# Memory attention with masked probabilities as the weights of the values product, and a ones column for the row sums

## The chip, the cores and the metric

The kernel runs on one core of a Trainium2 chip. The metric is the time of one execution on the device in microseconds (us). The time before is the median of three runs, 1568.24 us (1566.88 to 1571.79). A profile shows one execution, instruction by instruction; its span runs from the first to the last instruction.

## The reference

Two blocks alternate over x (2048 tokens of 512 numbers), each twice: A, B, A, B. Each is added to its input after a layer norm. Everything is stored in bf16.

```
def A(x, mem0):                       # 32 heads of 128, 64 segments of 32 tokens, 8 memory tokens
    mem = mem0
    for s in range(64):
        h = concat([mem, x[32 * s:32 * s + 32]])          # 40 tokens
        q, k, v = h @ Wq, h @ Wk, h @ Wv                  # per head
        scores = q @ k.T * 128 ** -0.5
        scores = where((idx[:, None] < 8) | (idx[:, None] >= idx[None, :]), scores, -1e9)
        o = (softmax(scores) @ v) @ Wo                    # summed over the heads
        mem = o[:8]                                       # memory of the next segment
        outs.append(o[8:])

def B(x):                             # linear attention, 32 heads of 16
    q, k, v = split(x @ wqkv); pq, pk = phi(q), phi(k)    # phi: t + 1 above 0, else exp(t), + 1e-6
    return (pq @ (pk.T @ v)) / (pq @ sum(pk) + 1e-6) @ wo
```

A memory token sees all 40 tokens, the others see those up to themselves. The memory makes the 64 segments of an A block a chain: segment s + 1 can't start its projections before segment s has its first 8 output rows.

## The kernel before, in words

**Blocks and segments.** `a_layer(0)` and `a_layer(1)` are the two A blocks, with 64 segments each. The B block of the tiles (128 tokens) is worked on beside them, by `b_in` (keys, values, sums) during the same layer and `b_out` (the result) during the next one; `b_mid` stands between. The weights Wq, Wk, Wv, Wo of A stay in SBUF.

**One segment.** Its tokens are 8 of memory and 24 new ones (`hT`); the last 8 tokens of each segment, the "left" ones, are projected for four segments at once (`left_block`, `left_values`: `vleft`). Heads are worked on in two halves `b`, four of them in four groups of 32 partitions each. `project` makes K, Q and V with 512-wide matmuls, four side by side in the four column parts of TensorE. `turned` evacuates K and Q and transposes them on VectorE in 32 x 32 blocks (line 2179). V is evacuated to `vimg`.

**Attention of the memory rows** (`mem_attention`, twice a segment, not in the last one: 252 times). The scores of all tokens lie in PSUM with the key tokens on the partitions (lines 2286 and 2294). ScalarE takes Exp (2301 for the memory rows, 2305 for the rest); VectorE spreads the memory rows' probabilities over the four parts with a mask (`Pm`, 2309). The row sums come from a matmul with a matrix of ones (`sums`), and ScalarE turns them into reciprocals with Ln and Exp (2320, 2322). The product takes the values as weights and the probabilities as moving data (`pvm`, through `tiled`, line 2060); VectorE multiplies it by the reciprocals into `oTb` (2334).

**Attention of the other rows** (`x_attention`, once a segment: 128 times). A mask (2352), sums by blocks with matmuls (2363, 2048), Ln and Exp (2366, 2368), scaling of the probabilities (2370, 2371), their spreading (`Pbx` 2374, `Pbl` 2379), the product with the values as weights (2060), and evacuations to `oTb` and `oTl` (1925 on ScalarE, 1926 on VectorE).

**Out.** `out_proj` multiplies `oTb` with Wo in 64 matmuls 256 wide (2424), adds the two halves of the heads (an evacuation to `outW`, and 2435), `next_mem` picks the memory rows (2452) and `residual` sends the other rows to `dx_sb` by DMA (1942), half of them through POOL's queue and half through SP's.

**Order.** Each instruction is a node with a key (layer, segment, name, number). A table `PLACE` gives each node a place in one list for all engines and, for those that ScalarE or VectorE can do (`ANY`, `evac`), the engine: "a" or "v". `schedule` sorts by it, gives out the eight PSUM banks and puts a semaphore wait where a node needs another engine's result. Each engine works through its part of the list in order, so an instruction that waits holds up everything behind it on its engine. Before, the numbers in the table are nanoseconds of a plan:

```
    (0, 10, 'mem0'): '155353 155412 155784 155903 156052 156645 157234 157542 157516 157918',
```

Of the kernel before, what the change touches and what calls it, by code (L numbers as in the profile page):

```python
# [6 lines left out]
F32 = mybir.dt.float32  # L7
F32R = mybir.dt.float32r
ACTF = mybir.ActivationFunctionType
ALU = mybir.AluOpType  # L10
# [1789 lines left out]
def _build_kernel(nc, A_x, A_mem0, A_Wq, A_Wk, A_Wv, A_Wo, A_seg_len, B_wqkv, B_wo, out):  # L1800
# [47 lines left out]
    st_sb = sb("st_sb", [128, 2, 16], F32)  # L1848


    ARENA_N = 35344
    arena = sb("arena_sb", [128, ARENA_N])
    off = [0]

# [1055 lines left out]
```

## Time and profile before

| | |
|---|---|
| Median of three runs | 1568.24 us (1566.88 to 1571.79) |
| Span of the profiled execution | 1565.9 us |
| Around the span, by the median of the runs | 2.3 us |
| Instructions in the profile | 97,746 |
| PE / PEld / DVE / ACT / POOL busy | 1514.7 / 822.9 / 1223.1 / 990.8 / 196.6 us |
| Granted TensorE clock | 0.998 |
| First 50 us: loading of the weights | 346 GB/s |
| Layers: stretches 50 to 770 and 810 to 1510 us | 720 and 700 us for 62 or 63 segments each |

The page has no time of the profiled execution other than its span; what lies around it is worked out from the runs. PE is TensorE's matmuls, PEld its weight loads, DVE VectorE, ACT ScalarE, POOL GpSimd and SP the queue of SyncE. A row of a group gives the line, the engine, the operation, out<-in by the names of the tiles, out<-in in partitions x elements, the count, and behind the bar the busy time in us and the mean of one in ns, then the idle time of the engine before them and what ended it. A row of the timeline gives the start in us, how long it took, and the count of merged instructions. `pb` is PSUM; `arena_sb` holds most of the tiles above. The records of instructions overlap: the next one may begin in its engine's pipe before the one before it has ended.

### The profile page before, as it was taken

What the parts mean: (1) busy time and instruction counts of PE and PEld (TensorE: products, weight loads), DVE (VectorE), ACT (ScalarE), POOL (GpSimd) and SP (SyncE); (2) the same over time, 40 slices, a digit from 0 to 9 for tenths busy, and PEclk for the clock granted to TensorE, in tenths of its full rate; (3) what the DMA queues carried; (4) which work ended last, traced back from release to release, by engine and by line L of the source; (5) the groups of instructions that cost most, each with busy time, mean ns of one, the idle gap of its engine ahead of it and who ended that gap; (6) DMA issues with size and microseconds to landing.
All of it is one profiled execution on the core that took longest, in us unless ns stands there. A gap on an engine that the chain in (4) does not pass through costs nothing.

```text
span 1565.9 us, 97746 instructions
## 1 busy us (share of the span) xinstructions
PE 1514.7 (97%) x48653; PEld 822.9 (53%) x40845; DVE 1223.1 (78%) x3520; ACT 990.8 (63%) x3059; POOL 196.6 (13%) x396
## 2 busy tenths in 40 slices
PE   6999999999999999999999999999999999999997
PEld 3455555555555555555545555555555555555454
DVE  4677878887777778777887878788888778777867
ACT  2566666666676666565666667656676666676666
POOL 2011110111111011111111110111111011111010
PEclk9999999999999999999999999999999999999999
DMA  9311000101000010101311100111001010111134
GB/s 383 96 31 21 23 28 20 27 24 24 24 17 14 23 25 23 25 17 32 54 38 20 24 21 19 30 27 27 18 20 27 24 26 20 27 23 17 27 55 130
DMA packets 84869, 60.72 MB, mean 39 GB/s; under 512 B 64169, under 2 KB 78825, under 8 KB 82921
## 3 DMA queue, kind: packets, MB, share of 16 engines
q1 hardware_dynamic: 71144, 37.58, 9.5%
q0 software_dynamic: 13152, 16.75, 3.8%
q8 instruction: 351, 5.75, 1.5%
q14 instruction: 62, 0.50, 0.1%
q10 hardware_dynamic: 160, 0.14, 0.0%
HBM read 25.57 MB, written 11.67 MB: 24 GB/s over the span
## 4 chain that ended last, share of the span: by engine, by line
PE 87%; DVE 7%; ACT 3%; DMA 2%; issue 1%; SPq 0%; POOL 0%; DVEq 0%; POOLq 0%
PE pb L2160 32%; PE pb L2048 21%; PE pb L2424 18%; PE pb L2060 10%; PE pb L2603 2%; DVE arena_sb L1926 2%; PE pb L2286 1%; DMA dx_sb<-y_sb 1%; ACT arena_sb L1925 1%; PE pb L2363 1%; PE pb L2452 1%; DVE y_sb L2435 1%; DVE arena_sb L2179 1%; DVE st_sb L2098 1%; ACT outW_sb L1925 1%
## 5 line engine op out<-in xcount | busy, mean ns | idle before, releaser
L1925 ACT ACTIVATE arena_sb<-pb 128x512 bf16<-128x512 f32 (+5 forms) x1175 | 527.7, 481 | 314.7 <-PE pb L2048 144.5
L2160 PE MATMUL pb<-Wk_sb,arena_sb 128*32 128x512 bf16 x4192 | 363.3, 380 | 1.8 <-DVE arena_sb L1926 1.1
L1926 DVE CAST arena_sb<-pb 128x512 bf16<-128x512 f32 (+4 forms) x598 | 302.0, 514 | 79.2 <-PE pb L2048 40.3
L2424 PE MATMUL pb<-Wo_sb,arena_sb 128*32 128x256 bf16 x10368 | 338.2, 273 | 5.8 <-issue 2.3
L2179 DVE STREAM_TRANSPOSE arena_sb<-arena_sb 128x256 f32<-128x256 f32 x640 | 266.4, 433 | 56.9 <-ACT arena_sb L1925 49.8
L2424 PEld LDWEIGHTS pb<-Wo_sb,arena_sb 128*32 128x32 bf16 x10368 | 258.4, 96 | 48.4 <-DVE arena_sb L2334 15.9
L2060 PE MATMUL pb<-arena_sb 128*32 128x128 bf16 (+2 forms) x10800 | 267.6, 208 | 11.2 <-DVE arena_sb L1926 3.9
L1942 POOL DMA_DIRECT2D dx_sb<-y_sb x246 | 124.8, 511 | 1146.1 <-DVE y_sb L2435 675.2
L2160 PE MATMUL pb<-Wq_sb,arena_sb 128*32 128x512 bf16 x3088 | 258.9, 380 | 1.1 <-issue 0.3
L2060 PEld LDWEIGHTS pb<-arena_sb 128*32 128x32 bf16 x10800 | 186.9, 95 | 135.9 <-issue 29.3
L2160 PE MATMUL pb<-Wv_sb,arena_sb 128*32 128x512 bf16 x2560 | 252.2, 380 | 0.0
L2048 PE MATMUL pb<-Wv_sb,arena_sb 128*32 128x512 bf16 x2560 | 252.1, 380 | 0.0
L2160 PEld LDWEIGHTS pb<-Wk_sb,arena_sb 128*32 128x32 bf16 x4192 | 112.3, 96 | 190.4 <-issue 99.4
L2048 PE MATMUL pb<-Wq_sb,arena_sb 128*32 128x512 bf16 x2032 | 198.9, 379 | 0.0
L2160 PEld LDWEIGHTS pb<-Wq_sb,arena_sb 128*32 128x32 bf16 x3088 | 83.8, 96 | 95.3 <-issue 42.0
L1925 ACT ACTIVATE outW_sb<-pb 64x256 f32<-64x256 f32 x137 | 51.7, 377 | 109.3 <-PE pb L2424 94.4
L2334 DVE TENSOR_TENSOR arena_sb<-pb,arena_sb 128x128 bf16<-128x128 f32 x252 | 73.2, 291 | 42.5 <-ACT arena_sb L2322 14.0
L2435 DVE TENSOR_TENSOR y_sb<-pb,outW_sb 64x256 bf16<-64x256 f32 x162 | 68.7, 424 | 46.4 <-ACT outW_sb L1925 41.3
L2374 DVE TENSOR_TENSOR arena_sb<-arena_sb,bo_sb 128x512 bf16<-128x512 bf16 x256 | 102.8, 416 | 2.4
L2160 PEld LDWEIGHTS pb<-Wv_sb,arena_sb 128*32 128x32 bf16 x2560 | 70.3, 96 | 56.5 <-issue 32.8
L2048 PE MATMUL pb<-Wk_sb,arena_sb 128*32 128x512 bf16 x928 | 92.4, 379 | 0.0
L2305 ACT ACTIVATE arena_sb<-pb 128x160 bf16<-128x160 f32 x256 | 77.4, 305 | 15.6 <-PE pb L2286 7.9
(129 smaller groups left out, 1816.3 us busy)
## 6 DMA issues: line engine op xcount, KB each, us to landing
Wk_sb<-in_A_Wk_dram SPq DMA_DIRECT2D x1, 4096.0 KB, 13.4
Wq_sb<-in_A_Wq_dram SPq DMA_DIRECT2D x1, 4096.0 KB, 24.0
Wv_sb<-in_A_Wv_dram SPq DMA_DIRECT2D x1, 4096.0 KB, 33.6
Wo_sb<-in_A_Wo_dram SPq DMA_DIRECT2D x16, 256.0 KB, 7.4
xs_scratch<-x_sb POOLq DMA_DIRECT2D x32, 128.0 KB, 2.1
pq_scratch<-arena_sb POOLq DMA_DIRECT2D x27, 128.0 KB, 2.8
x_sb<-xs_scratch POOLq DMA_DIRECT2D x16, 128.0 KB, 2.3
dx_sb<-y_sb POOLq DMA_DIRECT2D x126, 12.0 KB, 1.7
```

What stands on the lines that cost most here:

```text
L1925: return e.activation(o() if callable(o) else o, i() if callable(i) else i, ACTF.Copy)
L1926: return e.tensor_copy(o() if callable(o) else o, i() if callable(i) else i)
L1942: add(eng, lambda e: e.dma_start(o, i), 0.55 if eng == "pool" else 0.66, reads=reads, writes=writes, dsem="%s%d" % (kind, k), lat=lat + (0 ...
L2048: return pe.add_instruction(mybir.InstMatmult(name=nc.get_next_instruction_name(), engine=mybir.EngineType.PE, ins=[pe.lower_ap(x), pe.low ...
L2060: r = pe.matmul(o[q], w[:, q], x, start=start, stop=stop, skip_group_check=True, tile_position=(0, 32 * j))
L2160: r = pe.matmul(o, blk[:, c, :], w, start=(c == 0), stop=(c == 3), tile_position=(0, 32 * j))
L2179: add("dve", lambda v: v.transpose(dst, src(img[:, k, :].bitcast(F32))), 0.445, reads=[("img", k, h) for h in range(2)], writes=[dkey])
L2305: add("act", lambda a: a.activation(PQ[:, r2, b, 64:224], tl.f32()[:, 64:224], ACTF.Exp, scale=SCALE), c_act(160), tiles=[tl], writes=[("P ...
L2334: add("dve", lambda v: v.tensor_tensor(oTb[:, s % NO, 16 * b:16 * b + 16, 0:8].rearrange("p (i j) q -> p j i q", i=4), heads(pv.f32()[:, 0 ...
L2374: add("dve", lambda v, b=b: v.tensor_tensor(Pbx[:, :, b, :].rearrange("p j (k x) -> p j k x", k=4), px[:, b, :].rearrange("p (k x) -> p k ...
L2424: r = pe.matmul(tl.f32()[32 * j:32 * j + 32, 0:256], oT[:, 4 * hh + n, :], Wo_sb[:, 8 * n + hh, 256 * d:256 * d + 256], start=(hh == 0 and ...
L2435: add("dve", lambda e: e.tensor_tensor(y, tl.f32()[a, 0:256], outW[c, v, :], ALU.add), c_dve(256), reads=[("outW", w), "y0"], tiles=[tl], ...
```

## The change

The row sums come along with the product. V's tiles get two more columns of ones per head (`vimg`, `vleft`: 130 columns for 128), set once by POOL. The product is turned round: the masked probabilities are the weights, 32 columns for each of the four column parts, and the values with their ones columns move, 130 wide. Its result has the tokens on the partitions and the row sum in column 128. VectorE takes the reciprocal of that column, VectorE or ScalarE scales the result by it (`scaled`), and VectorE transposes the scaled result in 32 x 32 blocks into `oTb` or `oTl`. The sums by matmuls, Ln, Exp and the spreading of scaled probabilities go; one mask of 640 columns for each half (`wx_sb`) takes the place of the mask, the scaling and the spreading. Wo is loaded in the order that the transposed result asks for, in 32 DMAs for 16, and `out_proj` reads its weights at every second element. `PLACE` is a new list: ranks in place of nanoseconds, with another order of all work and other choices between ScalarE and VectorE.

```
-    (0, 10, 'mem0'): '155353 155412 155784 155903 156052 156645 157234 157542 157516 157918',
...
+PLACE: 1538 entries with ranks from 0 to 13499
...
-    vimg = av(2 * 1024).rearrange("p (r x) -> p r x", r=2)
+    vimg = av(2 * 8 * 130).rearrange("p (r n x) -> p r n x", r=2, n=8)
+    vleft = av(2 * 8 * 130).rearrange("p (r b g d) -> p r b g d", r=2, b=2, g=4)
...
+    for b in range(2):
+        for j in range(4):
+            u = 16 * b + 4 * j
+            for i in range(4):
+                load(Wo_sb[32 * i:32 * i + 32, u:u + 4, :].rearrange("p (f e) m -> p f (e m)", f=2),
+                     A_Wo[8 * j + 4 * b + i].rearrange("(f x e) m -> x f (e m)", f=2, e=2), ("Wo", b, j, i),
...
         # mem_attention
-            add("pe", sums, 0.112, reads=[("Pm", k), "one"], tiles=[tl])
-            add("act", lambda a: a.activation(Rm[:, k, :], tl.f32()[:, 256:384], ACTF.Ln), c_act(128), tiles=[tl],
-            add("act", lambda a: a.activation(Rm[:, k, :], Rm[:, k, :], ACTF.Exp, scale=-1.0), c_act(128, 0, 1),
...
+            def pvm(pe):
+                for a, start in ((0, True), (1, False)):
+                    for i in range(4):
+                        w = Pm[:, k, 128 * a + 32 * i:128 * a + 32 * i + 32]
+                        m = vimg[:, r2, 4 * b + i, :] if a else vleft[:, g2, b, g, :]
+                        r = pe.matmul(pv.f32()[32 * i:32 * i + 32, 0:130], w, m, start=start, stop=not start, skip_group_check=True,
+                                      tile_position=(0, 32 * i))
+            add("dve", lambda v: v.reciprocal(rc, pv.f32()[:, 128:129]), 0.17, tiles=[pv], writes=[("Rm", k)])
+            scaled(omem[:, k, :].unsqueeze(1), lambda: pv.f32()[:, 0:128].unsqueeze(1), rc, 1, [("Rm", k)], [pv], [("om", k)])
+            add("dve", lambda v: v.transpose(oTb[:, s % NO, b, :, :, 0].rearrange("p h j q e -> p (h j) (q e)").bitcast(F32),
+                                             omem[:, k, :].bitcast(F32)), 0.232, reads=[("om", k)], writes=[("oTm", s % NO, b)])
+        def scaled(o, i, r, n, reads, tiles, writes):
+            def fn(e):
+                if hasattr(e, "activation"):
+                    for u in range(n):
+                        x = e.activation(o[:, u, :], i()[:, u, :], ACTF.Copy, scale=r[:, u:u + 1])
+                    return x
+                return e.tensor_tensor(o, i(), r.unsqueeze(2).to_broadcast([128, n, 128]), ALU.mult)
...
         # x_attention
+            for b in range(2):
                 add("dve", lambda v, b=b: v.tensor_tensor(
+                    Px[:, b, :].rearrange("p (n j x) -> p n j x", n=20, j=4),
+                    PQ[:, r2, b, 64:224].rearrange("p (n x) -> p n x", n=20).unsqueeze(2).to_broadcast([128, 20, 4, 8]),
+                    wx_sb[:, :].rearrange("p (n j x) -> p n j x", n=20, j=4), ALU.mult),
+            cols = lambda b, k, i: Px[:, b, 128 * k + 32 * i:128 * k + 32 * i + 32]
...
+                        for i in range(4):                      # for k in range(3), b in range(2)
+                            r = pe.matmul(pv.f32()[32 * i:32 * i + 32, 130 * k:130 * k + 130], cols(b, k, i),
+                                          vimg[:, r2, 4 * b + i, :], start=True, stop=True, skip_group_check=True,
...
+                scaled(ox, lambda pvv=pvv: pvv()[:, :, 0:128], rc, 3, [("Rx", b)], [pv], ["ox"])
...
+                    for k in range(3, 5):                       # the left rows, both halves in one bank
+                        for i in range(4):
+                            r = pe.matmul(pv.f32()[32 * i:32 * i + 32, 130 * b:130 * b + 130], cols(b, k, i),
+                                          vleft[:, g2, b, g, :] if k == 4 else vimg[:, r2, 4 * b + i, :], start=k == 3, stop=k == 4,
...
+            scaled(oleft, lambda: pvv()[:, :, 0:128], rc, 2, ["Rl"], [pv], ["ol"])
...
         # out_proj
-                            r = pe.matmul(tl.f32()[32 * j:32 * j + 32, 0:256], oT[:, 4 * hh + n, :],
+                            r = pe.matmul(tl.f32()[32 * j:32 * j + 32, 0:256], oT[:, b, f, n, :, :, e],
```

The built programs differ in these counts: TensorE 48,647 to 42,583 instructions, VectorE 3,522 to 4,108, ScalarE 3,063 to 2,634, POOL 400 in both, SP 376 to 392.

More of the change, by code (lines that the diff above doesn't have):

```diff
@@ L1962, in _build_kernel @@
         load(W[:, :, :], v, nm, t)
-    for i in range(4):
-        for n in range(4):
-            hs = slice(8 * n + 2 * i, 8 * n + 2 * i + 2)
-            load(Wo_sb[:, hs, :], A_Wo[hs].rearrange("h e d -> e h d"), ("Wo", i, n), 36.45 + 3.0 * i + 0.75 * n, "dWo%d" % i)
+    for b in range(2):
[4 more added lines that the diff above has]
+                     A_Wo[8 * j + 4 * b + i].rearrange("(f x e) m -> x f (e m)", f=2, e=2), ("Wo", b, j, i),
+                     36.45 + 6.0 * b + 1.5 * j + 0.375 * i, "dWo%d%d" % (b, j))
     P.count += 1
@@ L2313, in mem_attention @@
+                wm_sb[:, :].rearrange("p (n j x) -> p n j x", n=8, j=4), ALU.mult),
                 c_dve(256, 2), reads=[("PQm", r2, b), "wm"], writes=[("Pm", k)])
[L2315 to L2321 removed]
@@ L2344, in x_attention @@
             gl = slice(8 * g, 8 * g + 8)
-            pxl = PQ[:, r2, :, 64:224]
-            px = PQ[:, r2, :, 64:192]
-            p8 = PQ[:, r2, :, 192:224]
-            rx = Rx.rearrange("p (b x) -> p b x", b=2)
             pk = [("PQ", r2, 0), ("PQ", r2, 1)]
-            tl = P.tile()
-            add("dve", lambda v: v.tensor_tensor(pxl, pxl, mx_sb[:, :].unsqueeze(1).to_broadcast([128, 2, 160]), ALU.mult),
-                c_dve(320, 2), reads=pk + ["mx"], writes=[("Px", r2)])
-            def sums(pe):
-                for left in range(2):
-                    for j in range(4):
-                        q = slice(32 * j, 32 * j + 32)
-                        o = tl.f32()[q, 0:256].rearrange("p (b x) -> p b x", b=2)
-                        if left:
-                            r = again(pe, o[:, :, 96:128], bo_sb[:, q], p8, False, True, (0, 32 * j))
-                        else:
-                            pe.matmul(o, bo_sb[:, q], px, start=True, stop=False, tile_position=(0, 32 * j))
-                return r
@@ L2365, in x_attention @@
-            add("pe", sums, 0.137, reads=[("Px", r2), "bo"], tiles=[tl])
-            add("act", lambda a: a.activation(Rx, tl.f32()[:, 0:256], ACTF.Ln),
-                c_act(256), tiles=[tl], writes=["Rx"])
-            add("act", lambda a: a.activation(Rx, Rx, ACTF.Exp, scale=-1.0), c_act(256, 0, 1),
-                reads=["Rx"], writes=["Rx"])
-            add("dve", lambda v: v.tensor_tensor(px, px, rx, ALU.mult), c_dve(256), reads=["Rx"], writes=[("Px", r2)])
-            add("dve", lambda v: v.tensor_tensor(p8, p8, rx[:, :, 96:128], ALU.mult), c_dve(64),
-                reads=pk + ["Rx", ("Px", r2)], writes=[("PL", r2)])
+            last = s == NSEG - 1
@@ new lines, in x_attention @@
+                pvv = lambda pv=pv: pv.f32()[:, 0:390].rearrange("p (k x) -> p k x", k=3)
+                rc = Rc[:, 2 + 3 * b:5 + 3 * b]
+                add("dve", lambda v, rc=rc, pvv=pvv: v.reciprocal(rc.unsqueeze(2), pvv()[:, :, 128:129]), 0.18, tiles=[pv], writes=[("Rx", b)])
+                scaled(ox, lambda pvv=pvv: pvv()[:, :, 0:128], rc, 3, [("Rx", b)], [pv], ["ox"])
+                k0 = 0 if last else 1
+                add("dve", lambda v, b=b, k0=k0: v.transpose(
+                    oTb[:, s1, b, :, :, k0:k0 + 3].rearrange("p h j k q e -> p k (h j) (q e)").bitcast(F32),
+                    ox.rearrange("p k x -> p (k x)").bitcast(F32)), 0.366, reads=["ox"],
+                    writes=[("oTx", s1, b)] + ([("oTm", s1, b)] if last else []))
@@ new lines, in x_attention @@
+            pvv = lambda pv=pv: pv.f32()[:, 0:260].rearrange("p (b x) -> p b x", b=2)
+            rc = Rc[:, 8:10]
+            add("dve", lambda v: v.reciprocal(rc.unsqueeze(2), pvv()[:, :, 128:129]), 0.17, tiles=[pv], writes=["Rl"])
+            scaled(oleft, lambda: pvv()[:, :, 0:128], rc, 2, ["Rl"], [pv], ["ol"])
+            dst, wr = (oTb[:, s1, :, :, :, 3], []) if last else (oTl[:, g2, :, :, :, g], [("oTl", g2, b) for b in range(2)])
+            if last:
+                wr = [("oTx", s1, b) for b in range(2)]
@@ L2410, in out_proj @@
+            add("dve", lambda v: v.transpose(dst.rearrange("p b h j q e -> p b (h j) (q e)").bitcast(F32), oleft[:, :, :].bitcast(F32)),
+                0.3, reads=["ol"], writes=wr)
         def out_proj(oT, keys, urgent, end=False):
@@ L2422, in mm @@
                             k, d = divmod(j, 2)
-                            n = 2 * k + i
-                            r = pe.matmul(tl.f32()[32 * j:32 * j + 32, 0:256], oT[:, 4 * hh + n, :],
-                                          Wo_sb[:, 8 * n + hh, 256 * d:256 * d + 256], start=(hh == 0 and i == 0),
+                            n, f, e = 2 * k + (u + i) // 4, (u + i) // 2 % 2, (u + i) % 2
+                            r = pe.matmul(tl.f32()[32 * j:32 * j + 32, 0:256], oT[:, b, f, n, :, :, e],
+                                          Wo_sb[:, 16 * b + 4 * n + 2 * f + e, 256 * d:256 * d + 256], start=(hh == 0 and i == 0),
                                           stop=(hh == 7 and i == 1), tile_position=(0, 32 * j))
                     return r
-                add("pe", mm, 0.218, reads=[("Wo", hh // 2, n) for n in range(4)] + keys[hh // 4], tiles=[tl])
+                add("pe", mm, 0.218, reads=[("Wo", hh // 4, 2 * k + hh // 2 % 2, i) for k in range(2) for i in range(4)] + keys[hh // 4], tiles=[tl])
             k = int(w == NW - 1)
@@ L2467, in left_rows @@
         def left_rows(G):
[L2468 removed]
+            k = out_proj(oTl[:, G % 2], [[("oTl", G % 2, b)] for b in range(2)], False)
             rows_out(k, G, [(8 * g, 32 * g + 24, 8) for g in range(4)])
@@ L2524, in tokens @@
                 x_move(x_sb[:, slot(t), :], x_view[t], slot(t), [], [("x", slot(t))], "dxl", lat=8.5 if t <= 2 else 3.0)
+        at(-5, "ones")
+        for r in range(2):
+            add("pool", lambda p, r=r: p.memset(vimg[:, r, :, 128:130], 1.0), 0.3, writes=[("v", r, b) for b in range(2)] + ["pool"])
+            add("pool", lambda p, r=r: p.memset(vleft[:, r, :, :, 128:130].rearrange("p b g x -> p (b g) x"), 1.0), 0.3, writes=[("vl", r, b) for b in range(2)] + ["pool"])
         at(-4, "start")
```

130 lines of the change are left out of this document (47 added, 83 removed), and 3073 rows, old and new, of the table PLACE.

## The prediction

> **What bounds the kernel now.** I read the busy shares first, then the chain that ended last, then the two layers as stretches.
>
> ```profile
> PE 1514.7 (97%) x48653; PEld 822.9 (53%) x40845; DVE 1223.1 (78%) x3520; ACT 990.8 (63%) x3059; POOL 196.6 (13%) x396
> ...
> PE 87%; DVE 7%; ACT 3%; DMA 2%; issue 1%; SPq 0%; POOL 0%; DVEq 0%; POOLq 0%
> ```
>
> ```profile
> 50.00:770.00 720.00, 702.88 (x22933) 383.70 (x19224) 562.38 (x1649) 456.31 (x1434) 89.08 (x171) 1.00 0.11 26
> 770.00:810.00 40.00, 37.65 (x1012) 17.58 (x832) 33.81 (x89) 27.00 (x76) 7.86 (x12) 1.00 0.19 46
> 810.00:1510.00 700.00, 690.24 (x22594) 377.15 (x18836) 561.90 (x1632) 456.69 (x1431) 85.09 (x164) 1.00 0.11 23
> ```
>
> The last lines are the two attention layers and the linear attention between them; after each length come the busy times of PE, PEld, DVE, ACT and POOL. TensorE works nearly all the time and holds 87% of the chain; VectorE is second with 78 to 80% of each layer. So TensorE's work is what counts, if the other engines keep pace. What a group of four matmuls (four 32-column parts side by side) takes is read off the timeline:
>
> ```profile
> 699.77 1.04 PE L2160 MATMUL pb<-Wq_sb,arena_sb 128*32 128x512 bf16 x16
> ...
> 705.34 1.93 PE L2424 MATMUL pb<-Wo_sb,arena_sb 128*32 128x256 bf16 x64
> ...
> 706.24 0.42 DVE L2370 TENSOR_TENSOR arena_sb<-arena_sb 128x256 bf16<-128x256 bf16 x1 [0.42 <-ACT arena_sb L2368]
> 706.70 0.76 DVE L2374 TENSOR_TENSOR arena_sb<-arena_sb,bo_sb 128x512 bf16<-128x512 bf16 x2
> ...
> 707.38 0.22 DVE L2371 TENSOR_TENSOR arena_sb<-arena_sb 128x64 bf16<-128x64 bf16 x1
> ...
> 708.27 0.51 PE L2060 MATMUL pb<-arena_sb 128*32 128x128 bf16 x24
> ...
> 715.33 0.23 PE L2060 MATMUL pb<-arena_sb,one_sb 128*32 128x128 bf16 x4
> 715.39 0.23 PE L2048 MATMUL pb<-arena_sb,one_sb 128*32 128x128 bf16 x4
> ```
>
> Four 512-wide groups in 1.04 us, the last one running 0.38: (1.04-0.38)/3 = 0.22 us each. In the same way 256 wide: (1.93-0.27)/15 = 0.11; 128 wide: (0.51-0.22)/5 = 0.058. The product with the values (20 matmuls of L2060 at 715.71, 0.33 us) gives 0.031 for a group of 32 wide. Counts of the built program times these (4402 groups of 512 at 0.216, 2592 of 256, 2236 of 128, some 2800 small ones) come to about 1470 us of the 1566 us span. The other 95 us are waits and ends of matmuls; counted in the same way by stretches, some 17 lie in the first 50 us, 9 in the next 50, 13 behind 1510, and the rest is about 4% of each layer, or 0.45 us in a segment.
>
> The sum is made against the profiled execution, whose span is 1565.9 us; the timed runs lie 1 to 6 us above that and their median, 1568.2, 2.3 above it.
>
> **TensorE.** Removed per segment and half (252 times): the sums, two 128-wide groups (0.116), and values times probabilities, one 128-wide and four 32-wide groups (0.18); in their place two groups of 130, 0.118 at 0.059 each. That saves 0.18 us, 45 us in all. Removed per segment (128 times): the block sums L2363 and L2048, 0.11 + 0.06, and ten 128-wide groups (0.58); in their place ten groups of 130 (0.59). That saves 0.16 us, 20 us in all. Together 65 us on the engine that sets the end. No row shows 130 columns, nor four different value tiles moving side by side with probabilities as weights. The nearest are L2060 (0.058 for 128) and L2424, where the four parts read different columns of Wo, at 0.11 for 256, so the streams do not get in each other's way. With 0.055 to 0.065 for 1784 groups, the saving is 54 to 72 us. The output projection reads its weights at every second element now; the scores (L2286) do so already, and their weight loads take 95 ns like the 96 ns of L2424, so nothing.
>
> **VectorE.** Removed: 252 x 0.291 (L2334) = 73, L2352 41, L2370 54, L2371 28, L2374 106, L2379 36, copies of 384 and 128 columns 118 x 0.548 and 108 x 0.277 = 95; together 433. Evacuations handed to ScalarE, 90 x 0.685 and a few small ones: 70. Added: 256 masks of 640 columns. L2309 takes 0.281 for 256 and L2374 0.416 for 512, or 0.53 ns a column, so 0.48 each, 124 us (upper bound 0.80, at the 0.98 ns a column between the fp32 products L2823 and L2837). 636 reciprocals of one to three columns: none is in the trace; the smallest copy from PSUM (L2733, 4 columns) takes 0.158, L2334 0.291; I take 0.17, 108 us, since the size is the former's. 636 transposes of 64, 192 and 128 fp32 columns, between 0.158 and the 0.433 of 256 columns (L2179): 0.23, 0.37, 0.30 by the slope, 192 us. Scalings that the order gives to VectorE: 185 x 0.291, 156 x 0.548, 47 x 0.414 = 159. Small copies 8. Together 591, so VectorE gains some 88 us and goes from 1223 to about 1310 busy; in a layer from 78-80% to 87-89% of a shorter time. With the upper bounds (masks +82, reciprocals +77, transposes +83) it would be full.
>
> **ScalarE** loses Ln and Exp of the sums, 252 x (0.278+0.313) + 128 x (0.377+0.416) = 250 us, and 106 of copies; it gets 529 scalings of 128 columns, between 0.275 (copy) and 0.375 (the 0.1 that a column operand adds in L2834 against L2587), 145 to 198, and 60 of evacuations. Net -98 to -151. It has room, so this gives nothing by itself.
>
> **The path through a segment.** Behind the values product come now reciprocal, scaling, transpose: 0.17 + 0.29 + 0.23, two gaps of 0.03 between dependent instructions, 0.06 to TensorE, and 0.3 from the last group's start to VectorE's (0.22 and 0.08, as between 708.21 and 708.51): 1.1 us. Before it was sums, Ln, Exp, product: 0.06 + 0.3 + 0.28 + 0.03 + 0.31 + 0.05 + 0.29 + 0.06 = 1.4. In the new order of TensorE's instructions a common segment has between the first values product and the first Wo matmul two 512-wide groups, the second product and two more: 0.98 us, where about 1.05 is wanted behind the last group's 0.058; for the second half 1.31. So up to 0.07 us a segment is uncovered, 9 us over 126. If VectorE's queue is late by one more instruction, Wo waits for it, and behind Wo the copy, y, the memory and the next segment's K and Q.
>
> **The rest.** Wo comes in 32 loads of 128 KB in place of 16 of 256 KB, last in SP's queue; the bytes decide (383 GB/s in the first slice), and the first Wo matmul stands at 46.4 us, after the weights. The new masks and ones columns are set on POOL in that time too. The masks are covered by the weights' loading, and cost POOL's own 0.3 to 0.4 each, under 4 us, if that cover were gone. No other DMA is added; their places in SP's and POOL's queues move with the new order, and POOL's longest waits are for y. The first segments, with few other tasks, take 10.6 to 10.8 us at some 8.5 us of work; the shorter path may take 0.2 off three or four of them. Nothing for these.
>
> **Sum.** 1568.2 - 65 + 0 to 9, with the waits otherwise as long as now: 1503 to 1512; I take 1506.
>
> **Rivals.** (a) The new order has shorter waits as well. For it: 0.45 us a segment is there to be had, and ScalarE gets room. Against: VectorE gets fuller. Half of the layers' 50 us: 1480.
>
> (b) VectorE becomes the bound, if its instructions follow each other only when the one before is through. Its mean times by their counts come to 1374 us before, so 1462 after; 1030 instructions wait for the one before on the engine, 0.03 each, 31; and it idles 48 us at the start, between the layers and at the end: 1541, and 2 around it, 1543. Against it: the two L2374 take 0.76 together where one takes 0.416, and L2371 starts 0.08 before they end, so independent instructions overlap, and the sum would be some 300 us less. The Trainium skill (VectorE: DVE Perf Modes, "The DRAIN you can't avoid") says that the next instruction does not start until the pipe is empty and advises few instructions, which speaks against a change that adds 586; by that rule the 1543 would hold. These rows disagree with it here.
>
> (c) Slower: VectorE's queue puts a foreign instruction in front of the path. An evacuation of 512 columns (0.685) that is late ahead of the reciprocal makes Wo wait 0.69 + 0.07 us in each of 126 segments, 95 us: 1568 - 65 + 95 = 1598. It decides from 0.52 us a segment on. For it: VectorE at 88%, two reciprocals, scalings and transposes more in each queue. Against: in the common segment of the new order the three steps follow each other directly.
>
> (d) The four parts of a 130-wide group do not run side by side: 0.22 in place of 0.059, 1784 times, +287: 1790. L2424 speaks against it.
>
> **Numbers.** Forecast (1490 to 1530) 0.66; (a) 0.12; (b) 0.10; (c) 0.08; (d) 0.01; waits eat the whole gain and it stays within 0.3% (4.7 us, about what a measurement of this kernel can tell) 0.03. Faster: 0.66 + 0.12 + 0.10 = 0.88; slower 0.09. The range leaves out (c), (d), no change and the better part of (a): 1478 to 1550.
>
> **What would show it.** Right: groups of 130 at 0.055 to 0.065, PE still at 95% or more, some 85% of the chain, a segment 0.4 to 0.5 us shorter in both layers, VectorE near 1310 busy. Wrong: reciprocals over 0.25 us or masks near 0.8 us; waits of the Wo loads (now 15.9 us for L2334) that grow to 50 us or more behind the transposes; VectorE at 95% of a layer.

## The result, and the profile after

| | before | after |
|---|---|---|
| Median of the runs compared | 1570.86 us (1566.88 to 1574.19, six) | 1583.62 us (1575.69 to 1590.75, six) |
| Ratio to before | | 1.0086, 95% interval 1.0057 to 1.0114 |
| Span of the profiled execution | 1565.9 us | 1587.3 us |

The change made the kernel slower by 0.9%. The forecast was 1506 us, and the measured time lies above its range. The profiled execution of after took 1589.0 us and stands high among its runs, so sums over the two profiles have to reach 21.4 us, not the 12.8 between the medians.

The page of after, busy time of the engines and then the chain that ended last, by engine and by line:

```profile
PE 1481.1 (93%) x42589; PEld 770.0 (49%) x36301; DVE 1257.9 (79%) x4106; ACT 909.7 (57%) x2630; POOL 199.4 (13%) x396
...
PE 72%; DVE 10%; DMA 9%; SPq 3%; ACT 3%; issue 2%; POOL 0%; DVEq 0%
```

TensorE lost work, but its share of the chain fell from 87% to 72%. VectorE (10%), transfers (9%) and SP's queue (3%) took it over. The layers as stretches say the same, with busy times of PE, PEld, DVE, ACT and POOL behind each length:

```profile
50.00:770.00 720.00, 673.26 (x19532) 351.68 (x16592) 574.82 (x1910) 395.81 (x1179) 88.02 (x168) 0.99 0.10 24
...
810.00:1510.00 700.00, 676.70 (x19848) 353.11 (x16784) 570.66 (x1911) 438.21 (x1278) 85.32 (x167) 1.00 0.10 23
```

TensorE was idle for 17 of 720 us and 10 of 700 before; now it is idle for 47 and 23. VectorE is at 80 to 82%, not at the 87 to 89% forecast.

The durations were not the mistake. Groups of after, with busy us and mean ns of one behind the bar:

```profile
L2337 ACT ACTIVATE arena_sb<-pb,arena_sb 128x128 bf16<-128x128 f32 x529 | 162.3, 370 | 85.1 <-DVE arena_sb L2372 34.1
L2339 DVE TENSOR_TENSOR arena_sb<-pb,arena_sb 128x128 bf16<-128x128 f32 (+2 forms) x388 | 158.3, 409 | 9.4
L2353 DVE TENSOR_TENSOR arena_sb<-arena_sb,wx_sb 128x640 bf16<-128x640 bf16 x256 | 117.5, 472 | 3.8 <-ACT arena_sb L2305 2.9
L2375 DVE STREAM_TRANSPOSE arena_sb<-arena_sb 128x192 f32<-128x192 f32 x256 | 92.2, 360 | 14.4 <-ACT arena_sb L2337 12.4
```

The forecast had 145 to 198, 159, 124 and (0.37 each) 95 us for these.

**Segments.** The layers are chains of segments, so the useful unit is the time from one `next_mem` matmul (2452 before, 2443 after) to the next. TensorE's work in it is counted as in the prediction, groups by their pitch. A segment with over 1.2 us in which TensorE does nothing is called held here, the others plain.

| | before | after |
|---|---|---|
| First `next_mem` | 50.1 us | 57.1 us |
| Two layers | 1418.2 us | 1427.7 us |
| TensorE work in a segment, mean | 10.89 us | 10.42 us |
| Plain segments, mean period | 103 of 11.47 us | 87 of 11.17 us |
| Held segments, mean period | 21 of 11.28 us | 37 of 12.32 us |
| Ten shortest segments | 10.64 to 10.75 us | 10.87 to 10.90 us |

The work fell by 0.47 us a segment, 58 us in 124 segments, where the terms of the forecast give 0.52 a segment (2 x 0.18 + 0.16). Had every segment followed it, the layers would be 58 us shorter. Plain segments gave 0.30 of the 0.47, so 21 us of the saving are missing there (0.17 x 124). Held segments lie 1.15 us above plain ones now (37 x 1.15 = 43 us) and lay 0.19 below before (-4): 47 us. The first segment ends 7 us later; the stretch between the layers and the end add 5. -58 + 21 + 47 + 7 + 5 = 22, against the 21.4 of the spans. The experiments take up these terms.

### The profile page after: what moved, and what is told of

It reads as the page before. It is cut to its first block, busy times and chain, and to the rows that moved or that the text cites. A ratio compares the mean times of both kernels' runs of the same rounds, so it can differ in the third digit from the quotient of the medians.

```text
span 1587.3 us, 87186 instructions
## 1 busy us (share of the span) xinstructions
PE 1481.1 (93%) x42589; PEld 770.0 (49%) x36301; DVE 1257.9 (79%) x4106; ACT 909.7 (57%) x2630; POOL 199.4 (13%) x396
## 4 chain that ended last, share of the span: by engine, by line
PE 72%; DVE 10%; DMA 9%; SPq 3%; ACT 3%; issue 2%; POOL 0%; DVEq 0%
PE pb L2160 27%; PE pb L2048 17%; PE pb L2415 15%; DMA dx_sb<-y_sb 4%; SPq L1959 2%; PE pb L2060 2%; PE pb L2322 2%; PE pb L2365 2%; PE pb L2598 2%; DMA arena_sb<-arena_sb 1%; ACT arena_sb L1927 1%; PE pb L2286 1%; PE pb L2385 1%; DMA x_sb<-in_A_x_dram 1%; DVE arena_sb L2179 1%
## 5 line engine op out<-in xcount | busy, mean ns | idle before, releaser
L1927 ACT ACTIVATE arena_sb<-pb 128x512 bf16<-128x512 f32 (+4 forms) x959 | 483.4, 533 | 294.6 <-PE pb L2048 147.3
L2415 PE MATMUL pb<-Wo_sb,arena_sb 128*32 128x256 bf16 x10368 | 326.8, 275 | 18.1 <-issue 7.0
L2179 DVE STREAM_TRANSPOSE arena_sb<-arena_sb 128x256 f32<-128x256 f32 x640 | 257.2, 424 | 36.4 <-ACT arena_sb L1927 31.7
L2160 PE MATMUL pb<-Wq_sb,arena_sb 128*32 128x512 bf16 x3088 | 248.6, 379 | 0.4 <-ACT arena_sb L1927 0.2
L2337 ACT ACTIVATE arena_sb<-pb,arena_sb 128x128 bf16<-128x128 f32 x529 | 162.3, 370 | 85.1 <-DVE arena_sb L2372 34.1
L2048 PE MATMUL pb<-Wq_sb,arena_sb 128*32 128x512 bf16 x2032 | 199.3, 380 | 0.0
L1928 DVE CAST arena_sb<-pb 128x512 bf16<-128x512 f32 (+2 forms) x302 | 149.0, 497 | 55.7 <-PE pb L2443 24.7
L2339 DVE TENSOR_TENSOR arena_sb<-pb,arena_sb 128x128 bf16<-128x128 f32 (+2 forms) x388 | 158.3, 409 | 9.4
L2353 DVE TENSOR_TENSOR arena_sb<-arena_sb,wx_sb 128x640 bf16<-128x640 bf16 x256 | 117.5, 472 | 3.8 <-ACT arena_sb L2305 2.9
L2365 PE MATMUL pb<-arena_sb 128*32 128x130 bf16 x3072 | 105.0, 220 | 2.4 <-issue 1.3
L2375 DVE STREAM_TRANSPOSE arena_sb<-arena_sb 128x192 f32<-128x192 f32 x256 | 92.2, 360 | 14.4 <-ACT arena_sb L2337 12.4
```

Of the source, the lines that this page charges most:

```text
L1927: return e.activation(o() if callable(o) else o, i() if callable(i) else i, ACTF.Copy)
L1928: return e.tensor_copy(o() if callable(o) else o, i() if callable(i) else i)
L2048: return pe.add_instruction(mybir.InstMatmult(name=nc.get_next_instruction_name(), engine=mybir.EngineType.PE, ins=[pe.lower_ap(x), pe.low ...
L2160: r = pe.matmul(o, blk[:, c, :], w, start=(c == 0), stop=(c == 3), tile_position=(0, 32 * j))
L2179: add("dve", lambda v: v.transpose(dst, src(img[:, k, :].bitcast(F32))), 0.445, reads=[("img", k, h) for h in range(2)], writes=[dkey])
L2337: x = e.activation(o[:, u, :], i()[:, u, :], ACTF.Copy, scale=r[:, u:u + 1])
```

## The experiments

Three theories stood on the result. Theory 1: the 32 loads of Wo hold up the start. Theory 2: in the new order VectorE stands in front of transfers that have not landed, and each such wait holds the whole chain. Theory 3: the path from one memory to the next sets the pace, and it has become longer, not shorter; TensorE work off this path counts for little. Ratios are to the kernel before, with 95% intervals; differences between runs of different chips are taken by the ratios.

### The start: Wo in fewer or spread loads

Stretches of before and then of after; the last two columns are the busy share of the 16 DMA engines and GB/s:

```profile
40.00:50.00 10.00, 9.65 (x273) 4.57 (x205) 7.33 (x20) 4.49 (x14) 0.00 (x0) 0.94 0.63 200
50.00:60.00 10.00, 9.04 (x285) 4.81 (x236) 7.08 (x22) 5.31 (x17) 0.00 (x0) 1.00 0.14 43
```

```profile
40.00:50.00 10.00, 4.31 (x100) 1.57 (x68) 4.63 (x14) 2.61 (x7) 0.00 (x0) 0.95 1.07 238
50.00:60.00 10.00, 6.82 (x124) 3.22 (x104) 2.90 (x9) 0.86 (x2) 0.00 (x0) 0.54 0.31 79
```

Before, the loads were through by 46 us. After, all DMA engines are busy for the whole of 40 to 50 us and yet move 238 GB/s, where the old loads moved 349 to 351 (40 to 44 us). TensorE stands still meanwhile, and then works at a granted clock of 0.54, the mean of the second stretch. The first try went back to 16 loads, each with four heads at once:

```
-    load(Wo_sb[32 * i:32 * i + 32, u:u + 4, :]..., A_Wo[8 * j + 4 * b + i]...)           # 32 loads, 32 partitions each
+    load(Wo_sb[:, u + 2 * f:u + 2 * f + 2, :]..., A_Wo[8 * j + 4 * b:8 * j + 4 * b + 4, 64 * f:64 * f + 64, :]...)   # 16 loads, 128 partitions each
```

> The changed kernel with Wo loaded in 16 DMAs of 256 KB that each write all 128 partitions, in place of 32 DMAs of 128 KB that each write 32 partitions. Same data, same order. Theory 1 (the 32-partition loads are slow: the stretches 40 to 50 us moved 229 to 243 GB/s, against 349 to 351 in the kernel before, with the DMA engines as busy): Wo is there some 5 us earlier, the first memory selection (57.1 us after the start now, 50.1 before) moves to 50 to 52 us, and the time falls by 5 to 7 us, to about 1577. Rival (the first segment is late for another reason, TensorE's order or the new setting of masks): the selection stays at 56 to 57 us and the time at 1583.

Measured: 1607.99 us, 1.0234 (1.0212 to 1.0256). It became worse, which neither side of the expectation had, and the profile of this run says why:

```profile
50.00:60.00 10.00, 2.09 (x32) 1.06 (x32) 0.00 (x0) 0.00 (x0) 0.00 (x0) 0.50 0.26 101
```

The DMA share is 0.26, about 4 of 16 engines, at 101 GB/s, and the first `next_mem` comes at 79.5 us instead of 57.1. The source pattern has an outermost dimension of four. The Trainium skill (DMA: Bandwidth & Descriptors, "Why a DMA increments its semaphore by 16 and not by 1") says that a transfer uses the largest number of engines, up to 16, that divides the slowest dimension on both sides; this trace agrees, with 0.26 for 4 of 16. The theory's place was right, its cure was not. The second try keeps the 32 loads and sends every other one through POOL's queue:

```
+    load(..., "dW%s%d%d" % ("op"[i % 2], b, j), i % 2 > 0)        # where true: through POOL's queue
```

> The changed kernel in which every second load of Wo (the odd quarters of 32 partitions) goes through POOL's queue, behind Wv, so that two quarters of the partitions are written at a time. Theory 1 (loads that write 32 partitions at a time are slow): more than 240 GB/s from 36 us on, Wo there 3 to 5 us earlier, the first memory selection at 52 to 54 us, 1578 to 1581. Rival (the rate has another cause, such as the rows of Wo in memory): no change, selection at 57, 1583.

Measured: 1581.64 us, 1.0073 (1.0053 to 1.0094). The first `next_mem` is at 54.4 us, 2.7 earlier, at 255 GB/s between 40 and 50 us. So a third of the 7 us comes back in the profile, too little for the intervals to part.

### The transfers that VectorE waits for

Waits of VectorE that a transfer ended (us in total, times, longest), before and then after:

```profile
DVE x_sb L2501 <- DMA dx_sb<-y_sb: 14.4, 14, 2.0
...
DVE st_sb L2098 <- DMA x_sb<-in_A_x_dram: 8.1, 2, 7.4
```

```profile
DVE x_sb L2492 <- DMA dx_sb<-y_sb: 34.9, 24, 3.3
...
DVE st_sb L2098 <- DMA x_sb<-in_A_x_dram: 15.4, 10, 3.5
```

From 22.5 to 50.3 us, and from 16 waits to 34. On the timeline of after, a held segment of 14.0 us (DVE's rows, then SP's):

```profile
424.37 0.43 DVE L2426 TENSOR_TENSOR y_sb<-pb,outW_sb 64x256 bf16<-64x256 f32 x1
...
430.33 0.43 DVE L2492 TENSOR_TENSOR x_sb<-x_sb,dx_sb 128x512 bf16<-128x512 bf16 x1 [1.57 <-DMA dx_sb<-y_sb]
...
437.03 0.69 DVE L2098 BATCH_NORM_STATS2 st_sb<-x_sb 128x6 f32<-128x512 bf16 x1 [1.20 <-DMA x_sb<-in_A_x_dram]
```

```profile
424.82 3.95 SPq L1944 DMA_DIRECT2D dx_sb<-y_sb  x5
```

The result of a segment (`y_sb`, 424.37) leaves by DMAs, and SP is busy until 428.77 issuing its five. Line 2492 needs the last rows of its tile and waits 1.57 us for them; the layer norm waits 1.20 us for its load. Everything behind these two on VectorE waits too, the reciprocals and scalings of the path included. Two runs cut these dependences without removing an instruction. The first adds the rows that the other buffer holds, of another tile, and in the first block A it normalizes the tile before, so that most of the transfers had long landed:

```
-    slot_t = slot(t)
+    slot_t = slot(t - back)                      # back = 1 in the first block A
-    ... dx_sb[0:n, G % 2, :] ...
+    ... dx_sb[0:n, (G + (0 < G < NT - 2)) % 2, :] ...
```

> The changed kernel in which the residual add takes the rows of the tile before (they landed four segments ago) and the layer norm of the first layer normalises the tile before, so that neither waits for a DMA; every instruction and DMA is still there, only the data differ. Theory 2 (the new order puts VectorE's instructions that need a DMA too close behind it, and VectorE's queue holds up everything): VectorE's waits for these rows (34.9 us) and for x (15.4 us) vanish, and the segments in which they lie, 13 to 14 us long against 11.2 for the others, become ordinary: 20 to 45 us less, 1540 to 1563. Rival (the path through each segment sets the pace, and those waits only took up slack): 1575 or more.

Measured: 1565.54 us, 0.9960 (0.9947 to 0.9974), 20 us below after. The two waits of VectorE are 13.7 us for 50.3:

```profile
DVE x_sb L2492 <- DMA dx_sb<-y_sb: 7.5, 3, 3.5
...
DVE st_sb L2098 <- DMA x_sb<-in_A_x_dram: 6.2, 3, 3.9
```

The second run also lets TensorE read its transposed tiles, for which it waited 8.2 us in after, from a part of Wo, in place of tiles that DMA transposes bring:

```
-    view = xT.rearrange("p c (g x) -> p c g x", g=4)
+    view = Wo_sb[:, 0, :].rearrange("p (c g x) -> p c g x", c=4, g=4)
```

> As the kernel named rows, and also: what the DMA transposes bring (the tiles for the linear attention and the rows of x for the segments) is not read, a weight that lies there since the start is read in its place; the transposes are still issued. Theory 2: TensorE's waits for the transposed tiles (8.2 us by the waits, in seven segments of 12.5 to 14 us) and those of the copies go too, another 8 to 20 us below rows: 1525 to 1550. Rival (path): no further change.

Measured: 1555.55 us, 0.9894 (0.9876 to 0.9911), 30 us below after. Held segments go from 37 of 12.32 to 31 of 11.40 us, and plain ones from 11.17 to 11.21. So 37 of the 47 us of the held segments were these transfers: 37 x 1.15 = 43 us above the plain ones became 31 x 0.19 = 6. The two layers together became 32 us shorter in the profile (1395.4 us). Theory 2 holds, though the two times lie 2.5 and 5.6 us above the ranges that were expected. It is not all: without most of these waits the kernel is still 50 us above the forecast.

### The path from V to Wo

Among the ten shortest segments after, one has 8.0 us of work and one has 10.4, and they take 10.88 and 10.87 us: in these the path alone sets the time, not the work. The end of such a segment before (10.65 us):

```profile
714.42 0.60 ACT L1925 ACTIVATE arena_sb<-pb 128x512 bf16<-128x512 f32 x1
...
714.92 0.28 ACT L2320 ACTIVATE arena_sb<-pb 128x128 f32<-128x128 f32 x1
...
715.06 0.43 PE L2060 MATMUL pb<-arena_sb 128*32 128x128 bf16 x28
715.22 0.31 ACT L2322 ACTIVATE arena_sb<-arena_sb 128x128 f32<-128x128 f32 x1
...
715.64 0.29 DVE L2334 TENSOR_TENSOR arena_sb<-pb,arena_sb 128x128 bf16<-128x128 f32 x1
...
715.98 1.93 PE L2424 MATMUL pb<-Wo_sb,arena_sb 128*32 128x256 bf16 x64
```

And after (10.88 us):

```profile
85.99 0.60 ACT L1927 ACTIVATE arena_sb<-pb 128x512 bf16<-128x512 f32 x1 [0.55 <-PE pb L2294]
86.05 0.65 DVE L1928 CAST arena_sb<-pb 128x512 bf16<-128x512 f32 x1
...
86.73 0.65 PE L2322 MATMUL pb<-arena_sb 128*32 128x130 bf16 x16 [0.66 <-DVE arena_sb L1928]
...
87.08 0.17 DVE L2327 RECIPROCAL arena_sb<-pb 128x1 f32<-128x1 f32 x1
...
87.28 0.29 DVE L2339 TENSOR_TENSOR arena_sb<-pb,arena_sb 128x128 bf16<-128x128 f32 x1
...
87.61 0.25 DVE L2329 STREAM_TRANSPOSE arena_sb<-arena_sb 128x64 f32<-128x64 f32 x1
87.77 0.13 DVE L2327 RECIPROCAL arena_sb<-pb 128x1 f32<-128x1 f32 x1
...
87.91 1.93 PE L2415 MATMUL pb<-Wo_sb,arena_sb 128*32 128x256 bf16 x64 [0.53 <-DVE arena_sb L2327]
```

The first row of each is the evacuation of V for the first half of the heads, in both on ScalarE: the table's entry for V in this segment ends in `710107a 710807v` before and in `511a 512v` after. By the code the first half's product waits for this evacuation and for its probabilities. Its row after names VectorE's evacuation, which is that of the second half, only because that ended last before it.

Before, V is out of PSUM at 715.02. Ln begins before that (714.92), and Exp ends at 715.53, about when the product does (715.49): sums, Ln and Exp need only the probabilities, so they run beside V and its product, and Wo begins 0.96 us behind V. After, V is out at 86.59, and reciprocal, scaling and transpose all need the product, which needs V: Wo begins 1.32 us behind V, 0.36 us more. The other parts of the shortest segments did not grow: from `next_mem` to the last group of V's projection they take 5.67 us for 5.80, and from the first Wo matmul to the next `next_mem` 2.87 us in both. 0.36 - 0.13 = 0.23, by which the shortest segments grew. The test takes the reciprocal off this path: the scaling takes the reciprocals of a segment before, and the reciprocal comes behind the transpose.

```
-    add("dve", lambda v: v.reciprocal(rc, pv.f32()[:, 128:129]), 0.17, tiles=[pv], writes=[("Rm", k)])
     scaled(omem[:, k, :]..., rc, 1, ...)
     add("dve", lambda v: v.transpose(oTb..., omem...), ...)
+    add("dve", lambda v: v.reciprocal(rc, pv.f32()[:, 128:129]), 0.17, tiles=[pv], writes=[("Rm", k)])
```

> The changed kernel in which the scaling of the memory rows uses the reciprocals of the segment before, and the reciprocal comes behind scaling and transpose on VectorE. All instructions are still there; the path from the values product to Wo is shorter by one reciprocal and its gap, 0.16 + 0.03 us. Theory 3 (in the ordinary segments the path from one memory to the next sets the pace: periods of 10.9 to 11.2 us at 10.4 to 10.7 us of TensorE work): 0.1 to 0.19 us less in most of 126 segments, 10 to 20 us less: 1563 to 1574. Rival (TensorE's or VectorE's work sets the pace of ordinary segments, the loss is in the DMA waits alone): within 4 us of 1583.

Measured: 1580.99 us, 1.0064 (1.0042 to 1.0085). The interval overlaps that of after, so by the time alone nothing is shown, and it lies on the side of the rival. Two of the shortest segments do move, from 10.88 to 10.67 us, which is about what the reciprocal and its gap take; the other eight of the ten shortest are at 10.77 to 10.84. The same edit with the transfers of the section above cut as well:

> rows_turns (1555.6 us) with the change of late_recip: the scaling of the memory rows uses the reciprocals of the segment before, and the reciprocal comes behind scaling and transpose. Theory 3 (with the DMA waits gone, the path from one memory to the next sets the pace of the segments): 0.1 to 0.19 us in each of 126 segments, 10 to 20 us less, 1536 to 1546. Rival (what late_recip showed, 3 us, is all there is: the path has slack): 1552 or more.

Measured: 1546.94 us, 0.9861 (0.9846 to 0.9875), 5 us below the run without it, where 10 to 20 were expected. The path counts where transfers don't cover it, but far from in full: 0.20 us in each of 124 segments would be 25 us.

### Work on the path and off it

On the kernel with the transfers cut, the next two take off work that is not on the path. The first shortens TensorE: the projections of the left tokens (V for four segments at once, Q and K) leave out three quarters of their last pass, 0.22 us a segment, 27 us in all.

```
+    if short and c == 3:
+        o, w = o[:, 0], w[:, 0]                  # 128 columns of 512, in the left tokens' projections
```

> rows_turns with less work on TensorE that is not on the path: in the projections of the left tokens (for four segments at once) the last quarter of each sum covers 128 of 512 columns. By the 0.216 and 0.058 us of such groups 0.157 us go per part, about 28 us of TensorE's 1481. Rival to theory 3 (TensorE's work sets the pace as before): 22 to 28 us less, 1528 to 1534. Theory 3 (path): TensorE's waits grow instead, at most 10 us less: 1546 or more.

Measured: 1554.31 us, 0.9906 (0.9891 to 0.9921): no gain for 27 us (the intervals leave room for 3). The shortest segments stay at 10.87, and the plain ones go from 11.21 to 11.18. The second shortens VectorE's masks from 640 to 128 columns:

```
-    Px[:, b, :]..., PQ[:, r2, b, 64:224]..., wx_sb[:, :]...
+    Px[:, b, 0:128]..., PQ[:, r2, b, 64:96]..., wx_sb[:, 0:128]...
```

> rows_turns with 128 of the 640 columns of the masks for the other rows (256 masks at 0.47 us; 0.13 to 0.16 remain): VectorE has some 80 us less to do, none of it on the path. Rival (VectorE's fill sets the pace): 20 us less or more, 1535 or below. Theory 3 (path): within 5 us of 1555.

Measured: 1554.34 us, 0.9911 (0.9892 to 0.9930). VectorE is busy 1193.7 us for 1257.6, and the time does not move. VectorE's fill isn't what bounds the kernel. The first edit in the kernel before, whose chain was 87% TensorE:

> The kernel before with the same cut as rt_lesspe: in the projections of the left tokens the last quarter of each sum covers 128 of 512 columns, about 28 us less work for TensorE off the path. Theory 3 (before, TensorE's work set the pace of a segment, 10.9 us of 11.4, and the path of 10.7 had room; after, the path sets it): most of the 28 us comes back here, 15 to 28 us less, 1541 to 1554, where rt_lesspe got none. Rival (the path sets the pace in both): 5 us less at most, 1564 or more.

Measured: 1568.07 us, 0.9983 (0.9974 to 0.9991): 2.7 us for 27. Here theory 3 in the form that was put on record fell, and its rival held: work of TensorE off the path did not bind the old kernel either. As the counterpart, as much work is taken off on the path, in the output projection of the memory rows: two of eight steps multiply 128 columns of 256.

```
+    m = 128 if urgent and hh in (5, 6) else 256
```

> rows_turns with less of TensorE's work on the path: the sixth and seventh of the eight steps of each segment's product with Wo cover 128 of 256 columns, 0.107 us less each by groups of 0.1105 and 0.057, 27 us in 128 segments. Theory 3 (the path sets the pace): 20 to 27 us less, 1528 to 1536, where the same amount off the path (rt_lesspe) gave nothing. Rival (neither TensorE nor the path, something else such as DMA or ScalarE): 5 us less at most, 1550 or more.

Measured: 1544.00 us, 0.9809 (0.9786 to 0.9832), 13 us below the run without it, where 20 to 27 were expected. The shortest segments go from 10.87 to 10.66 us. In the kernel before:

> The kernel before with the same cut on the path: the sixth and seventh of the eight steps of each segment's product with Wo cover 128 of 256 columns, 27 us in 128 segments. If the path sets the pace before the change too, as before_lesspe suggests: 20 to 27 us less, 1543 to 1550. If neither: 1565 or more.

Measured: 1561.51 us, 0.9931 (0.9915 to 0.9948): 10.8 us, with the shortest segments at 10.45 for 10.64.

| 27 us less TensorE work | in the kernel before | in the new one, transfers cut |
|---|---|---|
| off the path | 2.7 us | none |
| on the path | 10.8 us | 13 us |

Work on the path counts and work off it hardly does. But of the work on the path less than half came back, and of the reciprocal a fifth, so the path sets the pace in part of the segments only. What holds the others was not found.

### Other orders

If the place of each instruction is the matter, a better list may bring the gain. The first order was planned anew from the durations of after, with the spread loads of Wo; nothing else differs:

```
-PLACE: the ranks of after
+PLACE: ranks planned from the durations and DMA latencies of the profile of after
```

> The changed kernel with the same instructions, complete and unchanged but for the loads of Wo as in wo2, in a list that was planned anew from the durations in its own trace, with 2.3 us or more from the issue of a row's DMA to its landing, 3.6 for a transpose and 4.2 for x. Theory 2 (part of the loss is the order alone, which has too little room for DMAs): half of the 28 us of rows_turns comes back without leaving anything out, with 3 us from Wo: 1562 to 1572. Theory 3 says that no order of these instructions gets much below the 1548 to 1556 of rows_turns. Rival (the order is not at fault): 1580.

Measured: 1580.94 us, 1.0069 (1.0053 to 1.0086), no better than the spread loads alone (1.0073). The next one shortens the path instead: V's projection is made half by half, so that the first half leaves PSUM while TensorE makes the second, with an order planned for it.

```
-    for b, tl in enumerate(project(blk, bk, (Wv_sb, "Wv", 0, False), (Wv_sb, "Wv", 1, False), ...)):
+    for b, tl in enumerate([project(blk, bk, (Wv_sb, "Wv", h, False))[0] for h in range(2)]):
```

> As replanned, and V's projection in two halves, one after the other (four groups for the first half of the heads, then four for the second), where each step made both: the first half's V is there 0.43 to 0.86 us earlier, so its product, reciprocal, scaling and transpose are through before the second half's arrive. TensorE's matmuls are the same. Theory 3 (the path behind V's evacuation sets the pace): 0.2 to 0.35 us less in each of 124 segments, 25 to 43 us below replanned, 1525 to 1545. Rival (the path is not the bound): as replanned.

Measured: 1562.84 us, 0.9953 (0.9941 to 0.9965): 18 us below the replanned order, where 25 to 43 were expected, and faster than both kernels, with the whole computation. The shortest segment is at 10.48 us, below both. The order was planned for it, so the 18 us are not those of the shorter path alone. Last, the same kernel with an order that keeps more time behind each transfer:

> The whole computation, as in the run with V's projection split into its two halves, but with one more order of the work: the additions of the linear attention's rows, the layer norms and the transposed tiles are placed later behind the transfers that feed them (at least 3.7, 5.2 and 4.8 us behind their issue), so that VectorE should not stand in front of a transfer. Theory (the new order's transfers are tight, and each wait of VectorE for one becomes a long segment): VectorE's waits for these transfers, 25 to 29 us there, fall to under 12 us, and the time falls by 10 to 20 us from 1563 to 1543 to 1553. Rival (the path through a segment sets the rest, and such waits stand in segments that would be long anyway): the time stays within 5 us of 1563.

Measured: 1592.07 us, 1.0144 (1.0119 to 1.0168). Both expectations fell. The waits for `dx_sb` stayed (31.9 us for 28.6), and others grew; here VectorE's waits for ScalarE's evacuations of K and Q, without this order and then with it:

```profile
DVE arena_sb L2182 <- ACT arena_sb L1927: 59.4, 118, 1.9
```

```profile
DVE arena_sb L2182 <- ACT arena_sb L1927: 97.1, 151, 3.5
```

By these rows room for transfers was paid for in front of instructions on the path; no run tests that. Whether an order of the new kernel exists that has both is open.

## Why the prediction was wrong, point by point

**"So TensorE's work is what counts."** This step failed first. The cost in work was about right: a 130-wide group takes 0.06 us (0.29 for two, 0.23 for one on the timeline), and work in a segment fell by 0.47 us of 0.52. But the sum took the 65 us in full off the time. Work off the path returned 0 to 2.7 us of 27, even in the kernel before, and work on it 11 to 13. By the code and the timeline most of what the change removed (row sums by matmul, block sums, the product of the other rows) lay off it; these parts were not tried one by one. The 97% busy and 87% of the chain misled: a chain that is followed back from the last instruction runs through an engine that is merely kept full by work that can slip. The Trainium skill (Perfetto Trace Analysis, "Identifying the Most-Contended Engine") calls matmul busy time a poor measure of how close a kernel is to its limit and prefers the rate of arithmetic reached and the busy share of weight loads; here the latter stood at 53% before and 49% after, which agrees with TensorE not being the limit.

**"The path through a segment."** 1.1 us against 1.4 was forecast, 0.3 shorter; behind V it became 0.36 longer. Each of its durations came out (0.17, 0.29, 0.25 for 0.17, 0.29, 0.23). The mistake was to put sums, Ln and Exp on the old path, though they need only the probabilities and ran beside V. For the same reason "the shorter path may take 0.2 off" the first segments had the wrong sign: 0.23 were added. The reciprocal, 0.20 of the 0.36, was worth 5 us where transfers did not cover it; the whole was not tried alone.

**"With the waits otherwise as long as now."** The largest single loss: transfers that VectorE met too early held the chain, 30 us by the run that cut them. The text looked at the DMAs that the change adds, and said of the others only that their places move. It did not look at how far each transfer's reader stands behind its issue in the new order.

**Wo's loads, "the bytes decide".** They did not: 32 partitions at a time moved 238 GB/s for 350, and the start took 7 us longer.

**VectorE near 1310 busy.** 1258 was measured. Masks, scalings and transposes came out as priced. All durations of VectorE in the two profiles add up to 1385 us before (rival (b) had 1374) and 1449 after, 64 more for the 88 forecast; the rest of the 52 is that records overlap by 191 us for 162. Rival (a) fell, since the waits grew. Rivals (b) and (c) made VectorE the bound or put a foreign evacuation ahead of the path. The first fell with the masks, 64 us less for nothing. Of the second, the sign was right, but what VectorE stood behind was transfers, and the three steps of the path follow each other directly. (d) fell with the 0.06. The rule of the Trainium skill that (b) cites (VectorE: DVE Perf Modes, "The DRAIN you can't avoid") has an exception in the same section, which the prediction left out: a next instruction that is not held starts earlier. The trace of after fits the exception: the reciprocal at 87.77 starts 0.09 us before the transpose of 87.61 has ended.

None of the signs of being wrong that the text names appeared (reciprocals 0.16 us, masks 0.47, VectorE at 82% of a layer, 38 us of waits of Wo's weight loads behind the transposes and reciprocals). Those of being right did fail: TensorE at 93% and 72% of the chain, for 95% and 85%.

**How the losses add up.** The 65 us of gain in the sum and the 13 of loss between the medians leave 78 to explain. The transfers are 30 and the start 7 by the profile. The rest, some 41, is work that did not count and the longer path; the runs show both, but not how they share it. The change brought new instructions and a new order together, and no run has the new instructions in the old order, so how much of the transfers' 30 us any order would cost is open too. Plain segments keep 0.47 us in which TensorE does nothing (0.32 before), and none of the runs with the whole computation brought that down.

## What to carry to other kernels

In a recurrence, draw the path from one state to the next from the timeline of a segment that has little other work, and ask of each edit whether it is on that path. An engine at 97% with a full chain may only be filled with work that can slip; taking 2% of such work away is a cheap test, and here it would have stopped the forecast. When a change comes with a new order, measure for every transfer how long its reader stands behind its issue.

## What the hardware did that was not expected

- Loads of Wo with 32 destination partitions moved 229 to 243 GB/s with all DMA engines busy (share 1.03 to 1.11 between 40 and 50 us), loads of 128 partitions 349 to 351 at the same share. The first moved pieces of 2 KB (two rows of Wo), the second of 1 KB. The larger pieces are not the reason by the load below, which wrote 128 partitions in pieces of 2 KB: 101 GB/s are 25 for each of 4 engines, where 238 are 15 and 350 are 22 for each of 16.
- A load whose outermost source dimension is four had a DMA share of 0.26 and moved 101 GB/s.
- In after TensorE had nothing to do from 48 to 52 us, and its granted clock was 0.50 from 50 to 58 us; before it was 1.00 there.
